# A new written order for the head of a retention-plus-gated-MLP kernel: blocks first, V products in four steps, splitting shared out over three engines

## The chip, the core and the metric

The kernel runs on one core of a Trainium2 chip. The metric is device time in microseconds of one execution. The kernel before has a median of 406.89 us over three runs (404.96 to 407.62). The profiled execution was a run of 406.76 us, whose span from the first to the last instruction is 404.8 us; the 1.96 us between them lie around the span.

## The reference

A linear attention with decay (retention) feeds a gated MLP that also mixes along the sequence:

```python
for t in range(S):          # q, k, v: 4 batches, 8 heads, 768 steps, 64 wide
    state = gamma * state + k[t] (x) v[t]
    y[t]  = scale * (q[t] @ state)
x   = y, heads side by side                       # 4 x 768 x 512
h   = relu(x @ w_in);  u, v = halves of h         # 512 wide each
v_n = (v - mean) / sqrt(var + 1e-6)
v_s = w_spatial @ v_n + b_spatial                 # along the 768 steps
out = (u * v_s) @ w_out
```

The weights `w_in` and `w_out` come as float64. On the chip each is split into a high and a low part, and every product of that stage is three matmuls (high by high, high by low, low by high).

## The kernel before, in words

Each batch has six **groups** of 128 steps. A group `g` is loaded by `load_group` (word `G`, two DMAs of 512 KB into a `qv` tile, three buffers). Its scores are `s` (`q`, 32 small matmuls in the trace), masked on VectorE into `ws` (`j`); its values are scaled by the decay (`p`, GpSimd); in the first batch a running sum of k by v is kept in the PSUM tile `total` (`t`) and copied out by ScalarE (`k`); `y` makes the output products `x`; `E` brings them out of PSUM on VectorE into `xf`; `h` makes the high half `xh` (ScalarE) and `l` the low half `xl` (GpSimd).

The **weights** come in twelve blocks of 128 x 512: four of the V half of `w_in` (`winv_w`), four of its U half (`winu_w`), four of `w_out` (`wout_w`). `L` loads one (512 KB), `a` takes the absolute value on ScalarE, `c0`, `c1` and `c2` are five VectorE instructions (lines 180 to 200: two, two and one) that build the float32 parts, `H` writes the high part (ScalarE), and `R` the low part (`split_residue`). For blocks 0 and 1 `R` is three matmuls with an identity matrix into a PSUM tile `rud`, which ScalarE copies out (`A`); for the other blocks it is two GpSimd instructions (lines 132 and 217). A block lives in one of four `room` tiles while it is split.

For each of six row chunks there is a **V product** `V`: twelve matmuls in a row over the four blocks of `winv_w`. Then `r` (relu, ScalarE), `s` (statistics, VectorE), `w` (power -0.5, GpSimd), `n` (bias, VectorE) and `N` (normalised into `vnh`, ScalarE). All six `N` must be there before the first **spatial product** `sp` (lines 507 to 513). The MLP then goes through eight **units** (four column blocks by two halves): a U product `u` of twelve matmuls, `sp`, the gate (`t` on VectorE twice, `gh` on ScalarE, `gl` on GpSimd, lines 535 to 538), and the output product `o` of nine matmuls.

The **order** of the first batch's head is written by hand: `START` is a string of such words, emitted in that order, and with `fixed` set every instruction keeps its place on its engine. `START` of the kernel before ends with the two U products `u1` and `u0` and the last normalisation. Then comes `FIRST`, which holds the splitting of blocks 6 to 11 (`C6` to `C11`, six steps in one word) between the units (`I0` to `I7`) and the groups of the next batch (`S`, `X`, `G`). In `FIRST` the matmuls and the loads keep the written order and the scheduler places the rest. All loads are on SyncE's one queue, in the written order.

Of the kernel before, what the change touches and what calls it, by code (L numbers as in the profile page):

```python
# [9 lines left out]
F32 = mybir.dt.float32  # L10
# [13 lines left out]
START = (  # L24
    "v m L0 e G0 L1 L2 G1 L3 G2 L4 a0 c00 c01 q0 p0 c02 H0 j0 R0 a1 c10 t00 a2 y00 k00 c11 A0 t01 "
    "c20 y01 G3 L5 H1 k01 E0 q1 p1 j1 h0 a3 l0 t10 k10 c30 y10 t11 c21 y11 G4 K0 k11 p2 q2 E1 H2 a4 "
    "j2 h1 t20 l1 k20 c31 t21 y20 k21 p3 q3 c12 H3 y21 G5 K1 K2 L6 L7 B j3 R1 E2 t30 A1 c32 y30 h2 "
    "p4 k30 q4 c22 a5 t31 j4 y31 G6 k31 R2 t40 E3 k40 t41 c40 h3 R3 y40 k41 c50 q5 y41 j5 p5 V0 c41 "
    "c51 l2 H4 V1 r0 l3 c42 H5 E4 R4 t50 r1 c52 y50 k50 s1 V2 h4 R5 L8 L9 L10 L11 K3 K4 K5 s0 y51 "
    "r2 l4 V3 E5 w0 s2 h5 w1 l5 n0 n1 V4 N0 w2 r3 N1 n2 s3 N2 V5 w3 r4 n3 s4 N3 w4 u1 r5 n4 N4 s5 "  # L30
    "w5 u0 n5 N5"
)
FIRST = (
    "C6 C7 I0 C8 C9 I1 G7 Z5 C10 I2 S6 C11 G8 I3 X6 S7 G9 I4 X7 S8 W0 G10 I5 X8 S9 W1 G11 I6 X9 "
    "S10 W2 G12 V0 V1 I7 X10 S11 G13 N0 V2 N1 V3 N2 X11 G14 V4 N3 V5 N4 O7 N5"
)
# [10 lines left out]

BLOCKS = [0, 1, 2, 3, 4, 5, 6, 8, 7, 9, 10, 11]
STAGED = {i: (("vnh", "vnl")[i // 3], i % 3) for i in range(6)}
STAGED |= {i: ("vnl", i - 8) for i in range(8, 11)}  # L50
UNIT_BLOCKS = 2
WARM_UP = 10
# [3 lines left out]
def tile_retention_gmlp(  # L56
# [8 lines left out]
    mask: bass.AP,  # L65
    eye: bass.AP,
    vdecay: bass.AP,
# [4 lines left out]
    nc = tc.nc  # L72
# [23 lines left out]
    mask_t = wpool.tile([P, C], F32, name="mask_t")  # L96
    eye_t = wpool.tile([P, P], F32, name="eye_t")
    minus_t = wpool.tile([P, P], F32R, name="minus_t")
    vd_t = wpool.tile([P, NC, 2, NP], F32, name="vd_t")
# [28 lines left out]
    def load(dst, src):  # L128
        tc.keep_in_program_order(nc.sync.dma_start(dst, src))  # L129
# [3 lines left out]

    def pick(on_vector):
        return nc.vector if on_vector else nc.gpsimd

# [4 lines left out]
    ]  # L141
    doubles = [doubles[i] for i in BLOCKS]
    raws = {}

    def load_eye():
        load(eye_t, eye)
        keep(nc.scalar.mul(minus_t, eye_t, -1.0))

# [22 lines left out]
    def split_top(i):  # L171
        parts = raws.pop(i).bitcast(I32).rearrange("p (n w) -> p n w", w=2)
        a = rooms[i % 4] if fixed else rpool.tile([P, DM], F32, tag="xf", name=f"da{i}")[:, :]
        tc.keep_in_program_order(nc.scalar.activation(a, parts[:, :, 1].bitcast(F32), AF.Abs))
        halves[i] = [a, None, parts]
# [28 lines left out]

    def split_residue(i):
        hi, lo, _ = doubles[i]
        a, f, _ = halves.pop(i)
        if i < UNIT_BLOCKS:

            ps = ps_m.tile([P, DM], F32, tag="m", name=f"rud{i}")  # L210
            mm(ps, eye_t, f, start=True, stop=False)
            mm(ps, eye_t, a, start=False, stop=False)
            mm(ps, minus_t, hi, start=False, stop=True)
            halves[i] = ps
        else:
            keep(residue(nc.gpsimd, f, f, hi))
            keep(nc.gpsimd.tensor_tensor(lo, f, a, ALU.add))  # L217

    def split_copy(i):
        keep(nc.scalar.copy(doubles[i][1], halves.pop(i)))  # L220

    def split_double(i):
        for step in (split_top, split_exponent, split_sign, split_low, split_high, split_residue):
            step(i)

# [38 lines left out]

    def scale_values(g):
        vd = vd_t[:, g % NC].unsqueeze(3).broadcast_to([P, 2, NP, D])
        tc.keep_in_program_order(nc.gpsimd.tensor_tensor(values[g], values[g], vd, ALU.mult))  # L267

# [81 lines left out]
    def out_products(g, i):  # L350
        c = g % NC
        if i == 0:
            pool, tag = (ps_o, "o") if fixed else (ps_m, "m")
            outs[g] = [
                pool.tile([P, NP // 2, 2, C], F32, tag=tag, name=f"x{g}_{n}") for n in range(2)
            ]
        ts = outs[g]
        both = c > 0 or i > 0

        def part(hp, kept):  # L360
            w, m = (states, queries) if kept else (values, scores)
            for r in range(2):
                rows = place(hp, r)
                mm(
                    ts[hp % 2][ROWS[r], hp // 2, i],
                    w[g][rows, i, hp],
                    m[g][rows, i, hp],
                    start=not kept,
                    stop=bool(kept or not both),
                )  # L370

        for hp in range(0, NP, 2):
            for kept in range(1 + both):
                for n in range(2):
                    part(hp + n, kept)
        if i == 1:
            for kind in (queries, keys, values, naturals, scores):
                del kind[g]

# [20 lines left out]

    def out_half(g, low):
        b, c = divmod(g, NC)
        xh, xl = xhalf[b, c // TT]
        cols = slice((c % TT) * P, (c % TT) * P + P)
        if low:
            keep(residue(nc.gpsimd, xl[:, :, cols], outs.pop(g), xh[:, :, cols]))
        else:
            keep(nc.scalar.copy(xh[:, :, cols], outs[g]))  # L408
# [7 lines left out]

    def split3(pairs, ps):
        n = len(pairs)
        i = 0
        for (ah, al), (bh, bl) in pairs:  # L420
            for l, r in ((ah, bh), (ah, bl), (al, bh)):
                mm(ps, l, r, start=(i == 0), stop=(i == 3 * n - 1))
                i += 1
# [3 lines left out]

    def v_products(b, c):
        if b not in vn:
            vn[b] = [  # L430
                mpool.tile([P, NC, DM], F32R if b else F32, tag=tag, name=f"{tag}{b}", bufs=1)
                for tag in (("vnh", "vnl") if b else ("vnh",))
            ]
        xh, xl = xhalf[b, c // TT]
        cols = slice((c % TT) * P, (c % TT) * P + P)
        ps = ps_m.tile([P, DM], F32, tag="m", name=f"v{b}_{c}")
        split3(
            [
                ((xh[:, k, cols], xl[:, k, cols]), (winv_h[:, k], winv_l[:, k]))
                for k in range(KT)  # L440
            ],
            ps,
        )
        norm[b, c] = ps

# [60 lines left out]

    def mlp_spatial(b, j, half):
        dcol = slice(j * P, j * P + P)
        pp = ps_m.tile([P, DM], F32, tag="m", name=f"sp{b}_{j}_{half}")
        if b == 0:  # L510
            for s in range(NC):
                l, r = vn[b][0][:, s, dcol], whole_sp[half, s // 2][:, s % 2]
                mm(pp[:, :HALF], l, r, start=(s == 0), stop=(s == NC - 1))
        else:
            vh, vl = vn[b]
            split3(
                [
                    (
                        (vh[:, s, dcol], vl[:, s, dcol]),
                        (wsp_h[:, half, s], low_sp[half, s // 2][:, s % 2]),  # L520
                    )
                    for s in range(NC)
                ],
                pp[:, :HALF],
            )
        t = mpool.tile([P, HALF], F32, tag="t", name=f"t{b}_{j}_{half}")
        gh = mpool.tile([P, HALF], F32R, tag="gh", name=f"gh{b}_{j}_{half}")
# [39 lines left out]
    def item(b, i):  # L567
        if i == 0:
            mlp_u(b, *units[0])
        if i + 1 < NU:  # L570
            mlp_u(b, *units[i + 1])
        mlp_spatial(b, *units[i])
        if i > 0:
            mlp_out(b, *units[i - 1])
# [6 lines left out]
        "L": lambda b, g, n: load_double(n),  # L581
        "C": lambda b, g, n: split_double(n),
        "W": lambda b, g, n: split_spatial(n),
# [5 lines left out]
        "v": lambda b, g, n: [load(vd_t, vdecay), load(qg_t, qgroup), load(qd_t, qdecay)],  # L589
        "e": lambda b, g, n: load_eye(),  # L590
        "B": lambda b, g, n: load(bsp_t, b_sp),
        "q": lambda b, g, n: ret_scores(n),
        "p": lambda b, g, n: scale_values(n),
        "j": lambda b, g, n: ret_mask(n),
# [4 lines left out]
        "h": lambda b, g, n: out_half(n, False),  # L599
        "l": lambda b, g, n: out_half(n, True),  # L600
        "V": lambda b, g, n: v_products(0, n) if fixed else mlp_v(b + 1, n),
        "r": lambda b, g, n: v_relu(0, n),
# [6 lines left out]
        "H": lambda b, g, n: split_high(n),  # L609
        "R": lambda b, g, n: split_residue(n),  # L610
        "A": lambda b, g, n: split_copy(n),
    }

# [5 lines left out]
    nc.vector.memset(wz, 0.0)  # L619
    wps = ps_o.tile([P, DM], F32, tag="o", name="wps")  # L620
    for i in range(WARM_UP):
# [87 lines left out]
```

## Time and profile before

| what | value |
|---|---|
| median of three runs | 406.89 us (404.96 to 407.62) |
| the profiled execution | 406.76 us |
| its span | 404.8 us |
| instructions | 10218 |
| TensorE clock granted, mean | 0.977 |
| data moved | 41.55 MB |
| end of the third output product `o2` | 102.59 us |

The profile is one execution. A window row gives, for a stretch of the span, the busy microseconds of each engine, the granted TensorE clock and what the DMA engines did. A row of the chain of waits gives a start, a length and what the end of the program was waiting for then: a matmul row on TensorE followed by another means that TensorE ran on. A group row gives a line, an engine, an operation, the tiles, the count, busy microseconds and the mean of one in nanoseconds, and then the idle time just ahead of it.

### The profile page before, as it was taken

The numbers are of one execution on the slowest core, as the hardware profiler recorded it, in microseconds if no ns is written. First come the engines' busy times: TensorE is split into PE (matmuls) and PEld (weight loads), VectorE is DVE, ScalarE is ACT, GpSimd is POOL, SyncE is SP. The second block draws the span as 40 slices with busy tenths as digits, with TensorE's granted clock in tenths as the row PEclk, the third lists the DMA queues.
The fourth block names the chain that finished last, engine by engine and source line by source line (L and its number), as shares of the span: only waits on it lengthen the run. The fifth ranks groups of instructions, "written<-read, shape, count | busy, mean of one in ns | idle before, by whom it ended". The sixth has DMA issues, their size and how long they took to land.

```text
span 404.8 us, 10218 instructions
## 1 busy us (share of the span) xinstructions
PE 383.6 (95%) x4452; PEld 328.3 (81%) x4452; DVE 202.9 (50%) x433; ACT 127.6 (32%) x231; POOL 133.9 (33%) x128
## 2 busy tenths in 40 slices
PE   4976997799999998999999999999999999999996
PEld 2656785577777876899999988999999888999995
DVE  1799745997455665455543244454443246121122
ACT  2533355223132244622222144521132146311212
POOL 0359722667333333233333221243332222012010
PEclk8798999699999999999999999999999999999999
DMA  7989390000353314233335300233310000100202
GB/s 232 407 319 361 128 405 26 1 1 2 105 185 105 106 55 156 79 105 107 105 105 184 105 2 1 79 105 107 105 59 24 1 0 27 54 2 0 78 2 78
DMA packets 14012, 41.55 MB, mean 103 GB/s; under 512 B 1936, under 2 KB 2320, under 8 KB 13968
## 3 DMA queue, kind: packets, MB, share of 16 engines
q1 hardware_dynamic: 13968, 40.90, 28.5%
q8 instruction: 35, 0.57, 0.6%
q14 instruction: 9, 0.07, 0.1%
HBM read 34.61 MB, written 6.29 MB: 101 GB/s over the span
## 4 chain that ended last, share of the span: by engine, by line
PE 90%; ACT 2%; issue 2%; DVE 2%; POOL 1%; DMA 1%; SPq 1%; ACTq 0%; POOLq 0%
PE sp L124 26%; PE u L124 17%; PE o L124 16%; PE v L124 16%; PE x L124 6%; PE s L124 3%; PE d L124 3%; PE rud L124 1%; PE total L124 1%; DMA qv<-in_groups_dram 1%; DVE xf L391 1%; SPq L129 1%; ACT xh L408 0%; ACT vr L480 0%; POOL df L132 0%
## 5 line engine op out<-in xcount | busy, mean ns | idle before, releaser
L124 PE MATMUL u<-xh,winu_w 128*128 128x384 f32 x256 | 73.2, 349 | 4.9 <-POOL winu_w L217 3.9
L132 POOL TENSOR_TENSOR gl<-t,gh 128x384 fp32r<-128x384 f32 x31 | 32.3, 1042 | 132.8 <-ACT gh L537 124.6
L535 DVE TENSOR_TENSOR t<-sp,bsp_t 128x384 f32<-128x384 f32 (+1 forms) x34 | 18.0, 533 | 94.9 <-PE sp L124 94.9
L124 PE MATMUL o<-wout_w,gh 128*128 128x512 f32 x192 | 62.0, 404 | 0.0
L124 PE MATMUL v<-winv_w,xh 128*128 128x512 f32 x192 | 60.7, 397 | 0.6 <-ACT xh L408 0.6
L124 PEld LDWEIGHTS u<-xh,winu_w 128*128 128x128 f32 x256 | 47.5, 191 | 7.4 <-POOL winu_w L217 4.2
L124 PE MATMUL sp<-wsp_h,vnl 128*128 128x384 f32 x144 | 48.1, 334 | 0.0
L124 PE MATMUL sp<-wsp_h,vnh 128*128 128x384 f32 x144 | 48.1, 334 | 0.0
L124 PE MATMUL sp<-wsp_l,vnh 128*128 128x384 f32 x144 | 48.1, 334 | 0.0
L132 POOL TENSOR_TENSOR xl<-xf,xh 128x512 fp32r<-128x512 f32 x24 | 32.0, 1333 | 42.7 <-ACT xh L408 42.5
L537 ACT CAST gh<-t 128x384 fp32r<-128x384 f32 (+1 forms) x34 | 16.6, 493 | 92.6 <-DVE t L536 92.2
L124 PE MATMUL u<-xl,winu_w 128*128 128x384 f32 x128 | 43.5, 340 | 0.0
L124 PEld LDWEIGHTS v<-winv_w,xh 128*128 128x128 f32 x192 | 35.9, 190 | 8.7 <-ACT xh L408 1.0
L124 PEld LDWEIGHTS o<-wout_w,gh 128*128 128x128 f32 x192 | 35.8, 188 | 7.6
L391 DVE SCALAR_TENSOR_TENSOR xf<-x,qg_t,qd_t 128x128 f32<-128x128 f32 x96 | 27.0, 343 | 27.8 <-PE x L124 27.7
L124 PE MATMUL v<-winv_w,xl 128*128 128x512 f32 x96 | 37.7, 393 | 0.6 <-POOL xl L132 0.6
L124 PE MATMUL o<-wout_w,gl 128*128 128x512 f32 x96 | 37.7, 393 | 0.0
L124 PE MATMUL sp<-wst,vnh 128*128 128x384 f32 x96 | 33.6, 502 | 0.0
L267 POOL TENSOR_TENSOR qv<-qv,vd_t 128x512 f32<-128x512 f32 x24 | 28.4, 1182 | 15.7 <-DMA raw<-in_w_inv_dram 9.7
L124 PE MATMUL s<-qv 64*64 64x64 f32 x768 | 28.8, 226 | 4.0 <-DMA qv<-in_groups_dram 4.0
L124 PEld LDWEIGHTS s<-qv 64*64 64x64 f32 x768 | 26.2, 140 | 5.9 <-DMA qv<-in_groups_dram 4.4
L455 DVE BATCH_NORM_STATS2 bst<-vr 128x6 f32<-128x512 f32 x24 | 16.6, 693 | 28.6 <-ACT vr L448 28.6
(75 smaller groups left out, 623.6 us busy)
## 6 DMA issues: line engine op xcount, KB each, us to landing
qv<-in_groups_dram SPq DMA_DIRECT2D x48, 512.0 KB, 5.3
out_dram<-ot SPq DMA_DIRECT2D x23, 256.0 KB, 2.1
wst<-in_w_sp_dram SPq DMA_DIRECT2D x6, 384.0 KB, 7.4
raw<-in_w_inv_dram SPq DMA_DIRECT2D x4, 512.0 KB, 7.7
raw<-in_w_inu_dram SPq DMA_DIRECT2D x4, 512.0 KB, 7.6
raw<-in_w_out_dram SPq DMA_DIRECT2D x4, 512.0 KB, 7.7
bsp_t<-in_b_sp_dram SPq DMA_DIRECT2D x1, 384.0 KB, 8.8
qd_t<-in_qdecay_dram SPq DMA_DIRECT2D x1, 256.0 KB, 2.7
```

The source lines that it names most:

```text
L124: ins = nc.tensor.matmul(out, lhs, rhs, start=start, stop=stop, skip_group_check=shared)
L129: tc.keep_in_program_order(nc.sync.dma_start(dst, src))
L132: return eng.tensor_tensor(out, whole, high.bitcast(F32), ALU.subtract)
L267: tc.keep_in_program_order(nc.gpsimd.tensor_tensor(values[g], values[g], vd, ALU.mult))
L391: nc.vector.scalar_tensor_tensor(xf[:, hp], t[hp % 2][:, hp // 2].rearrange("p i c -> p (i c)"), qg_t[:, c, hp : hp + 1], qd_t[:, hp], ALU ...
L455: keep(nc.vector.bn_stats(st, norm[b, c][0]))
L535: nc.vector.tensor_tensor(t[:, c], pp[:, c], bsp_t[:, tc_], ALU.add)
L537: nc.scalar.copy(gh[:, c], t[:, c])
```

## The change

The strings `START` and `FIRST` are written anew. `START` now goes on until the third output product `o2` and the splitting of block 11, with the words `P` (a spatial product alone), `g` (the two VectorE steps of the gate), `f` (its high half, ScalarE), `d` (its low half, here always VectorE) and `o`. `FIRST` begins at the fifth unit. A word's first digit names the engine for `p`, `l`, `R` and `d`: 0 GpSimd, 1 VectorE, 2 ScalarE for `p` and `l`, and `R20` to `R31` are blocks 0 to 11 on VectorE.

- The identity, its negative, the two `rud` groups of matmuls and the copies `A` are gone. Blocks 0 and 6 to 11 get their residue on VectorE (two `TENSOR_TENSOR` each), blocks 1 to 5 on GpSimd.
- The decay scaling of group 0 is on VectorE, of group 1 on GpSimd, and of groups 2 to 6 on ScalarE as eight `ACTIVATE` of 128 x 64 each. The low halves of groups 1, 2 and 5 are on VectorE.
- The three gates inside the head have their low half on VectorE, and so has the fourth.
- `V` takes one block at a time: `V21` is chunk 2 with block 1, three matmuls. The steps of three chunks are placed between the score and output products of groups 2 to 5.
- The first load is block 0, then group 0, then the decay tables and the mask. The blocks are no longer permuted.
- The warm-up matmuls write to a tile of another PSUM pool.
- Of the next batch's groups, the score products of group 7 and the fifth U product come after `o2`; before, they came ahead of it.

```diff
-    "v m L0 e G0 L1 L2 G1 L3 G2 L4 a0 c00 c01 q0 p0 c02 H0 j0 R0 a1 c10 t00 a2 y00 k00 c11 A0 t01 "
...
+    "L0 G0 a0 c00 c01 H0 v c02 p10 m q0 L2 j0 t00 k00 y00 y01 t01 R20 G1 L1 p1 a2 G2 c20 E0 q1 h0 "
...
-    "C6 C7 I0 C8 C9 I1 G7 Z5 C10 I2 S6 C11 G8 I3 X6 S7 G9 I4 X7 S8 W0 G10 I5 X8 S9 W1 G11 I6 X9 "
...
+    "S6 I4 X6 S7 G9 W0 I5 X7 S8 G10 W1 I6 X8 S9 G11 W2 V0 V1 I7 X9 S10 G12 N0 V2 N1 V3 N2 X10 S11 "
...
-    def split_residue(i):
+    def split_residue(i, engine=None):
         hi, lo, _ = doubles[i]
         a, f, _ = halves.pop(i)
-        if i < UNIT_BLOCKS:
-
-            ps = ps_m.tile([P, DM], F32, tag="m", name=f"rud{i}")
-            mm(ps, eye_t, f, start=True, stop=False)
-            mm(ps, eye_t, a, start=False, stop=False)
-            mm(ps, minus_t, hi, start=False, stop=True)
-            halves[i] = ps
-        else:
-            keep(residue(nc.gpsimd, f, f, hi))
-            keep(nc.gpsimd.tensor_tensor(lo, f, a, ALU.add))
+        engine = engine or nc.gpsimd
+        keep(residue(engine, f, f, hi))
+        keep(engine.tensor_tensor(lo, f, a, ALU.add))
...
-    def scale_values(g):
+    def scale_values(g, engine=None):
+        engine = engine or nc.gpsimd
+        if engine is nc.scalar:
+            for i in range(2):
+                for hp in range(NP):
+                    v, f = values[g][:, i, hp], vd_t[:, g % NC, i, hp : hp + 1]
+                    keep(nc.scalar.mul(v, v, f))
+            return
...
-    def v_products(b, c):
+    def v_products(b, c, ks=range(KT)):
...
+        if not ks[0]:
+            norm[b, c] = ps_m.tile([P, DM], F32, tag="m", name=f"v{b}_{c}")
         split3(
-            [
-                ((xh[:, k, cols], xl[:, k, cols]), (winv_h[:, k], winv_l[:, k]))
-                for k in range(KT)
-            ],
-            ps,
+            [((xh[:, k, cols], xl[:, k, cols]), (winv_h[:, k], winv_l[:, k])) for k in ks],
+            norm[b, c],
+            start=not ks[0],
+            stop=ks[-1] == KT - 1,
         )
...
+        "R": lambda b, g, n: split_residue(n % 20, pick(n // 20)),
+        "P": lambda b, g, n: spatial_products(0, *units[n]),
+        "g": lambda b, g, n: gate_product(0, *units[n]),
+        "f": lambda b, g, n: gate_high(0, *units[n]),
+        "d": lambda b, g, n: gate_low(0, *units[n % 10], pick(n // 10)),
+        "o": lambda b, g, n: mlp_out(0, *units[n]),
```

How the order on the engines changes is shown at three places. The first is TensorE around the first V products (`v0_c` is chunk c, `x4_n` and `s5` are output and score products of groups 4 and 5, `rud` the identity products, `total` the running sum). The kernel before:

```order
L124 MATMUL rud1_429<-df1_185,eye_t_74 128x512
L124 MATMUL rud1_429<-room1_89,eye_t_74 128x512
L124 MATMUL rud1_429<-winv_w_82,minus_t_75 128x512
...
L124 MATMUL s5_570<-qv5_417 64x64 x16
L124 MATMUL x4_0_549<-ws4_308,qv4_307 64x64 x2
...
L124 MATMUL v0_0_606<-winv_w_82,xh0_222 128x512 x2
L124 MATMUL v0_0_606<-winv_w_82,xl0_223 128x512
```

The kernel after, from the scores of group 2 on:

```order
L122 MATMUL s2_298<-qv2_194 64x64 x16
L122 MATMUL s3_324<-qv3_267 64x64 x16
L122 MATMUL total_141<-qv2_194 64x64 x8
L122 MATMUL v0_0_362<-winv_w_80,xh0_200 128x512 x2
L122 MATMUL v0_0_362<-winv_w_80,xl0_201 128x512
...
L122 MATMUL s4_424<-qv4_355 64x64 x16
L122 MATMUL total_141<-qv3_267 64x64 x8
L122 MATMUL v0_1_459<-winv_w_80,xh0_200 128x512 x2
L122 MATMUL v0_1_459<-winv_w_80,xl0_201 128x512
...
L122 MATMUL s5_542<-qv5_522 64x64 x16
```

The identity products are gone, and a step of three V matmuls stands behind the scores of group 2, where the V products before began behind those of group 5.

The second place is the splitting of the later blocks. Before, GpSimd made their low parts between the gates:

```order
L132 TENSOR_TENSOR df7_886<-df7_886,wout_w_85 128x512
L217 TENSOR_TENSOR wout_w_85<-df7_886,da7_882 128x512
L132 TENSOR_TENSOR df8_911<-df8_911,winu_w_83 128x512
L217 TENSOR_TENSOR winu_w_83<-df8_911,da8_907 128x512
L132 TENSOR_TENSOR df9_922<-df9_922,wout_w_85 128x512
```

After, VectorE makes them in line with its other steps (`t` is a gate, `gl` its low half; lines 130 and 203 are the two residue steps):

```order
L193 SCALAR_TENSOR_TENSOR room0_86<-raw8_676,room0_86 128x512
L130 TENSOR_TENSOR df8_953<-df8_953,wout_w_83 128x512
L203 TENSOR_TENSOR wout_w_83<-df8_953,room0_86 128x512
L514 TENSOR_TENSOR t0_0_0_969<-sp0_0_0_946,bsp_t_77 128x384
L515 TENSOR_TENSOR t0_0_0_969<-t0_0_0_969,ur0_0_0_905 128x384
L184 SCALAR_TENSOR_TENSOR df10_976<-raw8_676,room2_88 128x512
L188 TENSOR_SCALAR room2_88<-df10_976 128x512
L130 TENSOR_TENSOR gl0_0_0_982<-t0_0_0_969,gh0_0_0_979 128x384
```

Two VectorE steps per block and one per gate are new there, and GpSimd has nothing between the last power of the normalisation and group 7.

The third place is SyncE's queue of loads behind group 6, after the change (`wst` is a piece of the spatial weights):

```order
L127 DMA qv6_666<-in_groups_dram 128x1024 x2
L127 DMA raw8_676<-in_w_out_dram 128x512
L127 DMA wst0_688<-in_w_sp_dram 128x768
...
L127 DMA raw7_85<-in_w_inu_dram 128x512
L127 DMA wst2_800<-in_w_sp_dram 128x768
L127 DMA bsp_t_77<-in_b_sp_dram 128x768
...
L127 DMA wst3_972<-in_w_sp_dram 128x768
```

`raw8` shares its buffer with blocks 3 to 5, so it waits for them to be split, and the first three pieces of the spatial weights, which stood ahead of such a wait before, now stand behind it.

## The prediction on record

> **What bounds the kernel now.** I read a table of windows first, cut where the work changes: the groups, the V products, the first unit, units two and three, the rest.
>
> ```profile
> core 0: us, PE busy (x) PEld busy (x) DVE busy (x) ACT busy (x) POOL busy (x), PEclk, DMA share, GB/s
> ...
> 8.87:40.09 31.22, 24.84 (x667) 19.66 (x667) 28.32 (x47) 12.02 (x25) 17.68 (x14) 0.88 0.96 363
> 40.09:59.51 19.42, 19.42 (x154) 15.68 (x154) 12.60 (x34) 8.55 (x14) 11.12 (x12) 0.96 0.69 261
> 59.51:76.62 17.11, 12.24 (x50) 9.98 (x49) 11.43 (x18) 6.44 (x11) 6.59 (x6) 0.87 0.11 45
> 76.62:102.59 25.97, 25.97 (x188) 18.36 (x189) 21.46 (x30) 7.80 (x15) 17.11 (x13) 0.95 0.00 1
> 102.59:404.80 302.21, 297.38 (x3393) 263.42 (x3393) 128.43 (x306) 90.64 (x164) 81.07 (x80) 1.00 0.22 75
> ```
>
> TensorE is the bound: 302.21 us after the third output product run almost without a hole, and the change leaves that work as it is. What can move is the head, up to 102.59. In the first row VectorE is busy 28.3 of 31.2 us and the DMA engines 0.96, while TensorE has holes; in the third TensorE stands still for 4.9 us. The view of TensorE's waits names the holes:
>
> ```profile
> PE s L124 <- DMA qv<-in_groups_dram: 4.0, 1, 4.0
> PE u L124 <- POOL winu_w L217: 3.9, 1, 3.9
> PE x L124 <- issue: 2.5, 1, 2.5
> ...
> PE total L124 <- issue: 1.6, 1, 1.6
> ```
>
> The first group's load, and a weight block that was split too late; "issue" is TensorE waiting for nothing that the profile shows.
>
> The chain of waits gives the price of each piece where it runs undisturbed, and of three that do not (the first `s`, the first `rud`, the `u` at 73.05):
>
> ```profile
> 3.53 5.29 DMA qv<-in_groups_dram
> ...
> 8.87 1.97 PE s L124 x32
> 10.84 3.88 PE rud L124 x5
> ...
> 24.86 0.62 PE total L124 x14
> ...
> 27.59 2.15 PE rud L124 x5
> ...
> 30.82 0.93 PE s L124 x32
> ...
> 32.22 0.47 PE x L124 x30
> ...
> 51.12 8.39 PE v L124 x36
> ...
> 73.05 3.57 PE u L124 x10
> ...
> 84.97 2.30 PE u L124 x12
> 87.28 3.87 PE sp L124 x12
> 91.14 2.09 PE o L124 x9
> ```
>
> Up to `o2` the kernel before has 8 `s` at 0.93 (7.4), 11 `total` at 0.62 (6.8), 12 half groups of `x` at 0.5 (6.0), 6 V chunks at 8.39/3 = 2.8 (16.8), 5 `u` at 2.30 (11.5), 4 `sp` at 3.87 (15.5), 3 `o` at 2.09 (6.3), and `rud` 3.88 + 2.15 (6.0): 76.3 us. From 8.87 to 102.59 are 93.7 us, so **17.4 us are lost**. By window: 8.4 among the groups, 1.0 in the V products, 6.3 from 59.51 to 76.62 (17.1, where two `u`, one `sp` and a third `u` make 10.8), 1.6 after.
>
> **The change part by part.** *Start.* Block 0 and group 0 are now the first three loads of a queue that issues one in some 0.45 us:
>
> ```profile
> 0.74 0.38 SPq L129 DMA_DIRECT2D vd_t<-in_vdecay_dram  x1
> 1.17 0.42 SPq L129 DMA_DIRECT2D qg_t<-in_qgroup_dram  x1
> ```
>
> The first half of group 0 takes the second place, at 1.2 us. With the 5.29 us to landing above, scores start at 6.5 instead of 8.87: 2.4 us.
>
> *TensorE work.* Up to `o2` it now has 7 `s`, 4 `u` and no `rud`: 6.5 + 6.8 + 6.0 + 16.8 + 9.2 + 15.5 + 6.3 = 67.1 us. The scores of group 7 (with the state product between them, 1.1) and the fifth `u` (2.3) are left for later; that is postponed and gains nothing. So with L for the time lost after the start, `o2` ends at 6.5 + 67.1 + L, and the span is 73.6 + L + 3.4 + 302.2 = 379.2 + L.
>
> *What L becomes.* Among the groups V steps fill holes, but the chain scores, mask, `x`, eviction is as long as it was and VectorE has more to do, so I keep the 8.4 us. The late block goes: blocks 4 and 5 are split ahead of the `u`, 6 and 7 well ahead of theirs; of 6.3 I keep 1.0, for the normalisation of the last chunk. Of the 1.6 after, 0.5 stays. In the V products 1.0 stays. ScalarE now scales groups 2 to 6 ahead of `total`. No row has a 128 x 64 `ACTIVATE`; the nearest are these:
>
> ```profile
> L289 ACT COPY ws<-total 128x256 f32<-128x256 f32 x11 | 4.1, 371 | 6.6 <-PE total L124 6.5
> L147 ACT ACTIVATE minus_t<-eye_t 128x128 fp32r<-128x128 f32 x1 | 0.3, 309 | 5.6 <-DMA eye_t<-in_eye_dram 5.6
> ```
>
> At most 8 x 0.309 = 2.5 us a group; with the slope between the rows (0.062 for 128 columns) 8 x 0.278 = 2.2. I take 2.3, against 1.13 on GpSimd. ScalarE has 12.0 busy of 31.2 us there, and `s` and V steps stand ahead of most of the sums: 1.0 us in all, between 0 (hidden) and 5 x 1.2 = 6. That makes L = 8.4 + 1.0 + 1.0 + 0.5 + 1.0 = **12**, and `o2` at 85.6. (The Trainium skill, "ScalarE: Activation LUTs", section "What ACT_TABLE_LOAD costs", gives 186 ns + 0.833 ns per column, 93 more for a pointer operand and 93 overlapped back to back: an estimate of 2.0 us a group, which would change the sum by nothing above 0.3 us a group.)
>
> *VectorE*, the second view of the same end. It takes residues of seven blocks and must keep up. Its prices, up to `o2`, and over the run for line 132:
>
> ```profile
> L200 DVE SCALAR_TENSOR_TENSOR room<-raw,room 128x512 f32<-128x512 uint32 x6 | 7.5, 1256 | 0.0
> L391 DVE SCALAR_TENSOR_TENSOR xf<-x,qg_t,qd_t 128x128 f32<-128x128 f32 x24 | 6.7, 341 | 3.6 <-PE x L124 3.5
> L309 DVE TENSOR_TENSOR ws<-s,mask_t 128x512 f32<-128x512 f32 x8 | 5.5, 682 | 1.1 <-PE d L124 1.0
> L182 DVE TENSOR_SCALAR room<-room 128x512 int32<-128x512 int32 x6 | 5.2, 862 | 0.2
> L180 DVE TENSOR_SCALAR room<-room 128x512 f32<-128x512 f32 x6 | 4.8, 806 | 8.0 <-ACT room L174 8.0
> L195 DVE TENSOR_SCALAR room<-df 128x512 int32<-128x512 int32 x6 | 4.5, 748 | 0.2
> L191 DVE SCALAR_TENSOR_TENSOR df<-raw,room 128x512 int32<-128x512 int32 x6 | 4.4, 727 | 0.1
> ...
> L455 DVE BATCH_NORM_STATS2 bst<-vr 128x6 f32<-128x512 f32 x6 | 4.1, 691 | 4.7 <-ACT vr L448 4.7
> ```
> ```profile
> L132 DVE TENSOR_TENSOR vnl<-vr,vnh 128x512 fp32r<-128x512 f32 x18 | 12.8, 725 | 9.2 <-ACT vnh L481 9.2
> ```
> ```profile
> 78.79 0.43 DVE L195 TENSOR_SCALAR da<-df 128x512 int32<-128x512 int32 x1
> 79.25 0.69 DVE L200 SCALAR_TENSOR_TENSOR da<-raw,da 128x512 f32<-128x512 uint32 x1
> 80.04 1.31 DVE L180 TENSOR_SCALAR da<-da 128x512 f32<-128x512 f32 x1
> ```
> ```profile
> 79.48 1.59 POOL L132 TENSOR_TENSOR df<-df,winu_w 128x512 f32<-128x512 f32 x1 [1.74 <-ACT winu_w L203]
> ```
>
> Undisturbed, a block's five steps cost 0.43 + 0.43 + 0.69 + 0.43 + 0.69 = 2.67 us; the means of blocks 0 to 5 add up to 4.40. The step at 80.04 shows why: it ends 0.28 us after GpSimd's instruction, three times its own length. Blocks 0 to 5 lost 10.4 us to some 28 us of GpSimd work. Until the third gate's low half VectorE now has the blocks but for the end of the last (30.2), 12 residue steps at 0.725 (8.7), 7 masks (4.8), six evictions (6.7), three low halves and one scaling (2.9), statistics and biases (some 7.3, 4.1 of it the row above), gates (3 x 3 x 0.55 = 5.0): 65.6 us. GpSimd has 18 us left beside it (14 steps near 1.3), at the same share 6.7 more. From about 6 us, with 4 us of waits, that ends at 82.3, and `o2` 2.4 later at 84.7. The two views agree within 1 us: both engines are nearly full, and VectorE has no slack left to give. (The Trainium skill, "SBUF — State Buffer", section "SBUF: two separate sides", calls the port pair of the two engines an exclusive lock, held for a whole instruction; the two rows agree.)
>
> *Queues.* `raw8` waits until VectorE ends block 5, at about 44 (from 6: six blocks 16.0, a residue, masks, evictions and the rest 13, the GpSimd share 6, waits 3). Behind it on SyncE stand the spatial weights, which land some 7 us after their issue:
>
> ```profile
> wst<-in_w_sp_dram SPq DMA_DIRECT2D x6, 384.0 KB, 7.4
> ```
>
> With six transfers in a row I allow 10 us, so 54, and the first `sp` comes near 58 (6.5, then 36.1 of groups and V products, 10.4 lost, two `u` 4.6). `wst3` to `wst5` wait for rooms that blocks 8 to 10 free near 76 and land by 84; the fifth `sp` comes past 90. I cost both at nothing; without that cover each is worth up to one landing, 7.4 us.
>
> **Sum.** 379.2 + 12 = 391.2 us of span, and 406.76 - 404.8 = 1.96 around it: **393.2 us**, against 406.76 of the profiled execution and a median of 406.89.
>
> **Rivals.**
> - *The lost time only moves.* L stays 17.4, because VectorE is late everywhere instead of one block once: 398.6. For it: 28.3 of 31.2 us busy already. Against: the 3.9 us wait is of one place that is gone.
> - *The holes are really filled.* The group stage loses only the two "issue" gaps (4.1) and L is 5: 386.2. For it: eight V steps stand there now. Against: TensorE waits in order, so a step helps only where its own inputs are earlier than the next score.
> - *VectorE stays in GpSimd's way.* If all twelve blocks cost 4.40, VectorE has 20.8 less 6.7 us more than I gave it, `o2` ends at 98.8 and the time is 406.4: no change. Against: beside blocks 6 to 11 GpSimd now has almost nothing.
> - *The clock falls (the slower side).* After the 3.9 us wait the `u` at 73.05 took 3.57 us for 10 of its 12 (4.3 against 2.30, 1.86 times), and the first `s` 1.97 against 0.93. If chopped V steps and short waits keep TensorE at that pace through groups and V products, V costs 14.4 and scores 7.2 us more: 414.8. It decides from about 14 us, where the gain is eaten. Against: the clock in the second window is 0.88 with holes of up to 2.5 us. (The Trainium skill, "TensorE: Matmul & The Clock Gate", section "What's actually happening", drops the clock after an idle window of about 3.4 us; by that the 3.9 us wait cost its slow stretch, which the trace shows, and the holes left would not.)
>
> **How the numbers follow.** Forecast 0.52; the lost time moves 0.22; holes filled 0.12; VectorE in the way 0.09; clock 0.05. Faster by over 1% (below 402.8, about what a measurement here can tell) are the first three: 0.86; within 1% the fourth, 0.09; slower 0.05. The range reaches to the filled holes below, and above past the moved loss toward the fourth: 386 to 402.
>
> **What would show it.** Right: scores start near 6.5; no `rud`; VectorE over 85% busy from 10 to 80; blocks 6 to 11 at 2.7 us each with GpSimd quiet; no wait on `winu_w` over 1 us; `o2` at 83 to 88; the stretch behind it as long as before. Wrong: `sp` waiting for `wst`, a granted clock under 0.9 from 40 on, VectorE's waits for TensorE growing, or over 2 us lost in the next batch, whose groups now run one place later.

## The result

The changed kernel takes 386.77 us (median of 4 runs, 386.46 to 387.37) against 405.92 of the kernel before on the same chip (4 runs, 404.57 to 407.62): a ratio of 0.9528, with a 95% interval of 0.9484 to 0.9572. Forecast were 393.2, in a range of 386 to 402. The profiled execution took 386.46 us, its span is 384.7, so 20.1 us less than before.

**The profile after.** The table of windows, cut where the work changes: the start, the groups (now with the V products of chunks 0 to 2 in them), the V products of chunks 3 to 5, the first four units up to `o2`, the rest.

```profile
core 0: us, PE busy (x) PEld busy (x) DVE busy (x) ACT busy (x) POOL busy (x), PEclk, DMA share, GB/s
...
5.50:41.30 35.80, 30.07 (x806) 25.57 (x805) 33.69 (x65) 22.19 (x64) 14.35 (x11) 1.00 0.77 291
41.30:49.69 8.39, 8.39 (x38) 6.96 (x38) 7.44 (x21) 6.42 (x16) 7.16 (x8) 1.00 0.83 272
49.69:79.77 30.08, 30.08 (x127) 22.27 (x129) 27.80 (x56) 12.29 (x22) 2.86 (x4) 1.00 0.49 171
79.77:384.70 304.93, 300.73 (x3469) 266.35 (x3469) 131.96 (x314) 92.50 (x167) 81.15 (x79) 1.00 0.21 74
```

TensorE is busy in every instant from 41.30 to 79.77, and its granted clock is 1.00 in every row, where before it was 0.88, 0.96, 0.87 and 0.95 in the four windows of the head. (Three of the four executions have a mean clock of 1.000; the fourth, 387.37 us, has 0.985.) VectorE is now the other full engine: 33.69 of 35.80 us, then 27.80 of 30.08.

The view of TensorE's waits, which showed 4.0 for the first group, 3.9 for `winu_w` and two "issue" gaps:

```profile
PE s L122 <- DMA qv<-in_groups_dram: 1.9, 3, 0.8
PE total L122 <- POOL qv L253: 1.7, 1, 1.7
PE total L122 <- DVE qv L253: 1.5, 1, 1.5
...
```

The wait on a weight block is gone. What is left in the head lies almost all ahead of 20 us: from there to the end of the groups TensorE is idle for 0.44 us.

```profile
5.50:20.00 14.50, 9.22 (x309) 8.27 (x310) 13.97 (x29) 6.51 (x18) 2.87 (x2) 1.00 1.03 396
20.00:41.30 21.30, 20.86 (x501) 17.30 (x499) 19.72 (x38) 15.68 (x47) 11.48 (x9) 1.00 0.59 221
```

The chain of waits from the last group on, with the third output product ending at 77.69 + 2.08 = 79.77 (102.59 before):

```profile
41.30 8.38 PE v L122 x36
49.69 4.18 PE u L122 x24
53.87 15.48 PE sp L122 x48
69.35 2.08 PE o L122 x9
71.43 2.09 PE u L122 x12
73.52 2.08 PE o L122 x9
75.60 2.09 PE u L122 x12
77.69 2.08 PE o L122 x9
```

Each row begins where the one ahead of it ends. The units' stage is pure matmul time.

**Where the 20.1 us came from**, by the boundaries of both profiles: the first scores start at 6.10 instead of 8.87 (2.8); from there to the first `u` it is 43.6 instead of 50.6 us (7.0; the `rud` work stood there for 6.0 before, but what its removal is worth is a question for the experiments); from the first `u` to the end of `o2` 30.1 instead of 43.1 us (13.0); behind that 304.9 instead of 302.2 (2.7 given back: the postponed `u`, scores and state product are 3.4, and 0.7 was gained at places that I did not trace).

### The profile page after: what moved, and what is told of

It is laid out like the page before. It is cut to its first block, busy times and chain, and to the rows that moved or that the text cites. A ratio compares the mean times of both kernels' runs of the same rounds, so it can differ in the third digit from the quotient of the medians.

```text
span 384.7 us, 10219 instructions
## 1 busy us (share of the span) xinstructions
PE 373.6 (97%) x4442; PEld 322.5 (84%) x4442; DVE 201.2 (52%) x455; ACT 135.3 (35%) x268; POOL 105.8 (28%) x105
## 4 chain that ended last, share of the span: by engine, by line
PE 88%; DVE 6%; DMA 3%; issue 1%; ACT 1%; POOL 1%; DVEq 0%; POOLq 0%; ACTq 0%
PE sp L122 28%; PE u L122 18%; PE o L122 17%; PE v L122 15%; PE x L122 5%; PE d L122 3%; PE s L122 2%; DMA qv<-in_groups_dram 2%; DVE xf L374 1%; DMA raw<-in_w_inv_dram 1%; DVE room L173 1%; DVE room L188 1%; DVE df L184 1%; PE total L122 1%; DVE room L175 1%
## 5 line engine op out<-in xcount | busy, mean ns | idle before, releaser
L122 PE MATMUL u<-xh,winu_w 128*128 128x384 f32 x256 | 71.4, 342 | 0.0
L130 POOL TENSOR_TENSOR gl<-t,gh 128x384 fp32r<-128x384 f32 x27 | 28.1, 1039 | 157.4 <-ACT gh L544 149.0
L542 DVE TENSOR_TENSOR t<-sp,bsp_t 128x384 f32<-128x384 f32 (+1 forms) x30 | 15.8, 531 | 94.2 <-PE sp L122 94.2
L122 PEld LDWEIGHTS u<-xh,winu_w 128*128 128x128 f32 x256 | 46.7, 188 | 1.5
L544 ACT CAST gh<-t 128x384 fp32r<-128x384 f32 (+1 forms) x30 | 14.5, 491 | 84.8 <-DVE t L543 84.5
L130 POOL TENSOR_TENSOR xl<-xf,xh 128x512 fp32r<-128x512 f32 x21 | 28.0, 1335 | 39.9 <-ACT xh L391 39.8
L122 PE MATMUL sp<-wst,vnh 128*128 128x384 f32 x96 | 31.8, 486 | 0.0
L122 PE MATMUL s<-qv 64*64 64x64 f32 x768 | 27.5, 221 | 1.9 <-DMA qv<-in_groups_dram 1.9
L122 PEld LDWEIGHTS s<-qv 64*64 64x64 f32 x768 | 25.2, 136 | 4.2 <-DMA qv<-in_groups_dram 2.1
L391 ACT CAST xh<-xf 128x512 fp32r<-128x512 f32 x24 | 14.9, 620 | 37.5 <-DVE xf L374 37.3
```

The source lines that it names most:

```text
L122: ins = nc.tensor.matmul(out, lhs, rhs, start=start, stop=stop, skip_group_check=shared)
L130: return eng.tensor_tensor(out, whole, high.bitcast(F32), ALU.subtract)
L542: nc.vector.tensor_tensor(t[:, c], pp[:, c], bsp_t[:, tc_], ALU.add)
L544: nc.scalar.copy(gh[:, c], t[:, c])
```

## The experiments

Each run is compared with the kernel before by its ratio, and with the changed kernel's 386.77 by its median. The changed kernel's own executions span 0.9 us, and the medians of the kernel before in the other comparisons lie within 0.4 us of the 405.92 above, so a difference of less than about 1 us says nothing. Where stages are compared, it is profile against profile, one execution each.

### The unit stage: the late block, and the clock behind it

**Block 6 early, in the kernel before.** One move in the old order (and block 6 keeps the buffer that it had):

```
START: ... V4 N0 [+ a6 c60 c61] w2 r3 N1 n2 [+ c62 H6] s3 N2 V5 ... N3 w4 [+ R6] u1 r5 ...
FIRST: [- C6] C7 I0 C8 C9 I1 ...
```

> The kernel before with one edit: the seventh block (the one whose lateness held up the third u for 3.9 us) is split some 10 us earlier, inside the head, on the same engines; all the rest of the old order stays. Theory (the unit stage lost its time to that one late block and to the slow clock behind it): 3.9 + 3 = 6 to 7 us faster than before, 398 to 400, so nearly half of the whole gain of the change. Rival (the next blocks are as late, the wait moves to blocks 7 and 8, since VectorE and GpSimd split them in each other's way): 1 to 3 us faster, 402 to 405, with a new wait of TensorE on a weight block.

Measured: 399.29 us, ratio 0.9824 (0.9783 to 0.9864): 7.0 us less than the 406.24 of before beside it. The units' window (five `u` here, as before) and what is left of waits on weight blocks in it:

```profile
57.45:94.35 36.90, 35.58 (x235) 26.03 (x237) 30.21 (x46) 13.45 (x25) 23.39 (x19) 1.00 0.13 53
```
```profile
PE o L124 <- POOL wout_w L217: 0.8, 2, 0.5
...
PE u L124 <- POOL winu_w L217: 0.5, 1, 0.5
```

Before, the same stretch took 43.08 us; it lost 6.2, as the theory had it. (This span is 8.4 shorter; the other 2 us lie ahead of the units, 1.4 of them ahead of the move: in this execution the groups ended at 38.73 instead of 40.09, with a hole of 1.71 us where it was 2.55, and the clock did not fall behind it.) The next blocks are late too, but by 1.3 us in all. So one late block, moved alone, is worth about a third of the whole gain: 6.2 of 19.1 us.

**The same wait filled with work, in the kernel before.**

```
         pu = ps_m.tile(...)
+        if b == 0 and half == 0 and j == 2:
+            for _ in range(24):
+                mm(pu[:, :HALF], winu_h[:, 0, :P], xh[:, 0], start=True, stop=True)
```

> The kernel before with 24 extra products of unit 0's weights into the third u's tile ahead of its own, some 4 us of TensorE work in the place of the 3.9 us wait; they are overwritten, so the result is the same. Theory (the wait itself and the slow stretch behind it are two losses: the u at 73.05 and the sp at 76.6 took some 3 us more than the same work elsewhere): with no standstill the slow stretch goes, 2 to 3 us faster than before, 402.5 to 404, and the granted clock stays at 1 there. Rival (the slow stretch has another cause, or the wait alone is the loss): 405 to 407, no change.

Measured: 404.14 us (10 runs), ratio 0.995 (0.9924 to 0.9977), so 2.1 us less although TensorE was given some 3 us more to do. The same two windows, the wait and what follows it, first of the kernel before, then of this one; the column behind the engines is the granted clock:

```profile
69.14:73.05 3.91, 0.00 (x0) 0.00 (x0) 3.88 (x3) 0.48 (x1) 3.86 (x3) 0.91 0.00 0
73.05:79.00 5.95, 5.95 (x15) 4.74 (x16) 5.66 (x8) 1.41 (x3) 2.93 (x2) 0.50 0.00 1
```
```profile
69.14:73.05 3.91, 2.87 (x18) 2.55 (x16) 3.88 (x3) 0.38 (x1) 3.81 (x3) 1.00 0.00 0
73.05:79.00 5.95, 5.95 (x24) 4.32 (x25) 5.66 (x8) 1.47 (x3) 2.91 (x2) 1.00 0.00 1
```

After the standstill the clock is at half for 6 us, in which 15 products get done; without it 24 do. (Of the wait 1.0 us stays empty.) From the block's arrival to the end of `o2` it is 27.0 us here (73.01 to 100.03) and 29.5 in the kernel before. The late block cost its wait and, behind it, some 2.5 us by the slow clock.

**The residues of blocks 6 to 11 and the gates' low halves on GpSimd again.** `R26 R28 R29 R30 R27 R31` become `R6 R8 R9 R10 R7 R11`, and `d10` to `d13` become `d0` to `d3`.

> The changed kernel with the residues of blocks 6 to 11 and the low halves of gates 0 to 3 on GpSimd again. Theory (VectorE has slack in the unit stage, since TensorE runs there without a hole; the steps taken from VectorE, 12 x 0.69 + 4 x 0.55 = 10.5 us, pay for the 6 us that GpSimd's work beside it costs): within 1% of the changed kernel, 386 to 389. Rival (GpSimd's place beside the blocks is what made them late before: their five steps go from 2.67 back to 4.40 us, six times 1.7 = 10.4, of which VectorE gets the 10.5 of residues back, but each residue takes 2.7 instead of 1.4 us, and a u or an output product waits for it): 391 to 396, with a wait on a weight block over 1 us.

Measured: 390.37 us, ratio 0.9594 (0.9569 to 0.9620), 3.6 slower than the changed kernel: too slow for the theory, just under the rival's range, and not by its wait either. No weight block is late; a gate's low half is, which stands behind the residues on GpSimd. TensorE's longest wait, and the windows around it:

```profile
PE o L122 <- POOL gl L130: 2.3, 1, 2.3
```
```profile
74.07:76.38 2.31, 0.00 (x2) 0.00 (x1) 2.21 (x3) 0.12 (x1) 2.31 (x3) 0.97 0.33 69
76.38:79.40 3.02, 3.02 (x7) 2.44 (x8) 0.36 (x1) 0.13 (x1) 2.78 (x2) 0.50 0.95 362
```

2.3 us of wait and 3 us at half clock, worth 1.5: that is 3.8 of the 4.0 us by which this span is longer. The move of residues and low halves to VectorE is worth this much, through the place in a queue and not through the blocks' own price. The two were moved together: what either is worth alone is not shown.

### The groups: who sets their length

**The V products whole again.** The twelve steps `V00` to `V23` stand together ahead of `a6`; all else as changed.

> The changed kernel with the V products of chunks 0 to 2 in one piece again: their twelve steps stand together where the last of chunk 0 stood, all else as changed. In the changed kernel eight of them run between 20 and 33 us, 0.68 us each. Theory (the steps fill holes of TensorE that VectorE's chain leaves, so out of their places they come on top): up to 8 x 0.68 = 5.4 us slower than the changed kernel's 386.8, so 389 to 392, and TensorE idle among the groups by as much more. Rival (the group stage is as long as VectorE's work, wherever TensorE's steps stand, and the twelve steps still fit ahead of its end): within 1 us, 386 to 388.

Measured: 391.68 us, ratio 0.9621 (0.9583 to 0.9659), 4.9 slower. From the chain, the twelve steps and the three chunks behind them (41.30 in the changed kernel):

```profile
35.66 8.43 PE v L122 x36
...
46.56 8.39 PE v L122 x36
```

The last three chunks start 5.3 us later, about the length of eight steps. In their place TensorE has a new hole,

```profile
PE x L122 <- issue: 2.0, 1, 2.0
```

and behind it the granted clock stands at 0.50 from 29 to 35.5 us. How the 5.3 divides between the steps and the clock is not told apart in this execution. The other three have a mean clock of 0.995 or 0.996; as an estimate, that leaves room for some 4 us at half clock, so for a loss of 2 us. They took 390.35 to 392.68 us, 3.6 to 5.9 more than the changed kernel, so at least 1.6 us are the place of the steps.

**The clamps of blocks 2 to 5 three times.**

```
-        tc.keep_in_program_order(nc.vector.tensor_scalar(a, a, TOP_MAX, TOP_MIN, ALU.min, ALU.max))
+        for _ in range(3 if 2 <= i < 6 else 1):
+            tc.keep_in_program_order(
+                nc.vector.tensor_scalar(a, a, TOP_MAX, TOP_MIN, ALU.min, ALU.max)
+            )
```

> The changed kernel with the clamp of blocks 2 to 5 run three times instead of once on VectorE (it changes nothing the second time): 8 more steps of 0.43 us, 3.4 us of VectorE work among the groups and nothing else. Theory (VectorE's chain sets the length of the group stage): 3 to 5 us slower, 390 to 392. Rival (TensorE's own order and the loads set it, VectorE has slack): within 1 us, 386 to 388.

Measured: 390.66 us, ratio 0.9622 (0.9591 to 0.9653), 3.9 slower; in the profile the groups end at 46.31 instead of 41.30:

```profile
5.50:46.31 40.81, 33.28 (x806) 28.99 (x805) 36.62 (x73) 22.27 (x64) 13.75 (x11) 0.87 0.69 254
```

3.4 us more on VectorE alone make the stage 5.0 us longer in this execution, the slowest of the four, with a clock of 0.87 in the window. Another of the four had a mean clock of 1.000 and took 389.46 us, 2.8 more than the changed kernel's executions at 1.000 (386.71, their median). So at full clock most of the 3.4 us arrives, and VectorE has next to no slack here. What is above that in the 5.0 may be the clock; it was not told apart.

**Later scores.** The words `v` and `m` (the decay tables and the mask) stand between `L0` and `G0`.

> The changed kernel with the decay tables and the mask loaded ahead of the first group, as before; block 0 stays first. The first scores come four issues later, some 1.9 us. Theory (the group stage is as long as VectorE's work, which starts with block 0, untouched): the groups end at most 0.5 us later, 386 to 388. Rival (the prediction's start term: scores that start later end later by as much): 1.9 us, 388 to 389.5, the groups' end near 43.2 instead of 41.3.

Measured: 387.59 us, ratio 0.9548 (0.9522 to 0.9574), whose interval holds the changed kernel's ratio: the 0.8 us between the medians are not clear of noise. In the profiles, first the changed kernel's and then this one, the scores start at 8.06 instead of 6.10, and the groups end 1.0 later, at 42.29:

```profile
6.10 1.35 PE L122 MATMUL s<-qv 64*64 64x64 f32 x32 [0.47 <-DMA qv<-in_groups_dram]
8.06 1.15 PE L122 MATMUL s<-qv 64*64 64x64 f32 x32 [2.42 <-DMA qv<-in_groups_dram]
```

In this pair half of the 2.0 us arrives: between the two expectations.

**The first group ahead of block 0.** `L0 G0` becomes `G0 L0`, and `p1` becomes `p11`.

> The changed kernel with the first group loaded ahead of block 0 and group 1 scaled on VectorE instead of GpSimd, an attempt to take away the first two waits (1.5 and 1.7 us of TensorE for scaled values). If these waits set the end: 1 to 2 us faster, 385 to 386. If VectorE does: it starts two issues (0.9 us) later and has 0.69 us more, less 0.4 from GpSimd: 1.2 us slower, 387.5 to 388.5.

Measured: 389.11 us (6 runs), ratio 0.9577 (0.9541 to 0.9614), 2.3 slower, and more than either expectation. VectorE's first step waits for block 0 until 8.04, where it was 5.46 in the changed kernel, which is the first row:

```profile
5.46 0.43 DVE L173 TENSOR_SCALAR room<-room 128x512 f32<-128x512 f32 x1 [4.32 <-ACT room L167]
8.04 0.43 DVE L173 TENSOR_SCALAR room<-room 128x512 f32<-128x512 f32 x1 [6.91 <-ACT room L167]
```

VectorE starts 2.6 us later and the last three V chunks 2.2 later (at 43.45). The expectation had 0.9 for the two issues; the block, issued at 1.65 instead of 0.74, also took 5.7 us to land instead of 4.0. Here the load that VectorE needs first is the one to issue first; the second edit, the scaling, was not run alone.

**The `rud` work put back.** The identity products for blocks 0 and 1 in the place of `R20` and `R1`, with a load `e` behind the third block's:

```
+        if i < 2:
...
+            mm(ps, eye_t, f, start=True, stop=False)
+            mm(ps, eye_t, a, start=False, stop=False)
+            mm(ps, minus_t, hi, start=False, stop=True)
...
+            keep(nc.scalar.copy(lo, ps))
+            return
```

> The changed kernel with the residues of blocks 0 and 1 made by identity products on TensorE again (with the load of the identity, its negative and the copy out on ScalarE). Before, these two took TensorE 6.0 us in all, 4.3 undisturbed. Theory (TensorE's holes among the groups are set by VectorE, so such work disappears in them, and VectorE is relieved of 1.4 us): within 1 us of the changed kernel's 386.8, 386 to 388. Rival (the prediction's sum: what TensorE is given is added to the end): 4.3 to 6 us slower, 391 to 393.

Measured: 393.15 us, ratio 0.9678 (0.9645 to 0.9711), 6.4 slower, but by neither reason: ScalarE stood behind its copy of the first `rud`, and VectorE behind ScalarE:

```profile
17.22 0.43 DVE L180 TENSOR_SCALAR room<-room 128x512 f32<-128x512 f32 x1 [7.78 <-ACT room L174]
```

So the run says only what a queue costs. A second run has the load behind the third group's, and `M`, `R20`, `A0` and `A1` (negative, products, copies) just ahead of the first V steps that need them.

> The residues of blocks 0 and 1 by identity products once more, now placed so that no queue stands behind them: the identity is loaded after the third group, its negative made and the products and copies put just ahead of the first V step that needs them (in the run before, VectorE stood still for 7.8 us behind ScalarE's copy of the first). Theory (TensorE's holes among the groups take such work): within 1.5 us of the changed kernel's 386.8, 386 to 388.5. Rival (what TensorE is given is added to the end): 4.3 to 6 us slower, 391 to 393.

Measured: 388.96 us, ratio 0.9571 (0.9534 to 0.9609), 2.2 slower. The two `rud`, the first V steps behind them (20.53 in the changed kernel) and the last three chunks:

```profile
20.39 2.15 PE rud L125 x5
...
23.15 2.15 PE rud L125 x5
...
25.30 0.70 PE v L125 x3
...
44.07 8.39 PE v L125 x36
```

The V steps are 4.8 us late at 25.30, the chunks 2.8 late at 44.07: the holes that follow take back 2.0. Well placed, putting the work back costs 2.2 us, not 6.0 and not nothing. That is net: the residue steps of block 0 leave VectorE and those of block 1 GpSimd.

### Who scales, who subtracts

**Groups 2 to 6 scaled on GpSimd.** `p22` to `p26` become `p2` to `p6`.

> The changed kernel with the values of groups 2 to 6 scaled on GpSimd (one instruction of 1.13 us) instead of ScalarE (eight of 0.34, some 2.0 us a group). The prediction priced ScalarE's longer scaling at 1.0 us on the path; by that it would be 1 us faster, 385 to 386.3. Rival (ScalarE has room, and GpSimd's work lengthens VectorE's by 0.37 us for each of its own): 5 x 1.13 x 0.37 = 2.1 us slower, 388 to 390.

Measured: 389.94 us, ratio 0.9608 (0.9579 to 0.9637), 3.2 slower: the rival's sign, within its range, and more than the 2.1 us of its sum. VectorE's steps do get longer: up to the third gate's low half its `df`, second `room` and `xl` groups (lines 184, 193 and 130, 26 steps in both kernels) take 20.4 us by their rows instead of 17.7.

**Three small pieces back on GpSimd.** `R20`, `l11`, `l12` become `R0`, `l1`, `l2`.

> The changed kernel with three pieces of the group stage back on GpSimd: the residue of block 0 and the low halves of groups 1 and 2. VectorE loses 4 steps of 0.69 = 2.8 us of its own; GpSimd gets 4 of 1.3 = 5.2 us. Theory (VectorE sets the group stage, and each us of GpSimd costs it 0.37): 2.8 - 1.9 = 0.9 us faster, 385.5 to 386.5. Rival (the chain through these pieces matters more than VectorE's load: a low half takes 1.3 instead of 0.7 us and V waits for it, and GpSimd's scaling of group 1 comes later): 1 to 3 us slower, 388 to 390.

Measured: 387.82 us (6 runs), ratio 0.9544 (0.9510 to 0.9577), whose interval holds the changed kernel's ratio: no difference that can be told. The profile shows one thing that neither theory named. VectorE's scaling of the first group, 0.69 us in the changed kernel, meets the residue on GpSimd, and the first sums come 1.1 us later for it (10.01 instead of 8.91). The changed kernel's step, then the two of this run:

```profile
8.18 0.69 DVE L253 TENSOR_TENSOR qv<-qv,vd_t 128x512 f32<-128x512 f32 x1
```
```profile
7.83 1.58 POOL L130 TENSOR_TENSOR df<-df,winv_w 128x512 f32<-128x512 f32 x1 [7.00 <-ACT winv_w L196]
```
```profile
8.35 1.61 DVE L253 TENSOR_TENSOR qv<-qv,vd_t 128x512 f32<-128x512 f32 x1
```

None of the edits to the changed kernel beats it.

## Why the prediction was right in sign and too high in time

The span was forecast as 379.2 + L with L = 12; it is 379.2 + 5.5. Most of the mechanisms stand; L was over-sized in nearly every term. The time came out at the rival "the holes are really filled" (386.2), but not by that rival's account, which left 4.1 us in two "issue" gaps: those gaps are gone, and 7.5 us are lost among the groups. Of the signs that the forecast named, `o2` at 83 to 88 failed (79.77); VectorE's share from 10 to 80 (64.8 of 70 us), the weight blocks in time and the clock of 1.00 from 40 on came as it said.

**Start.** 6.5 forecast, 6.10 measured. But the sum passed every us of it on to the end, and the profile of the run with later scores passes on only half: 1.0 of 2.0. What starts the stage as much is VectorE's first step, which the sum did not mention for itself.

**The groups** (8.4 kept, plus 1.0 for ScalarE's scaling, 9.4): measured are 35.2 us from the first score, of which 27.7 is work by the same prices, so 7.5 lost. Of these TensorE is idle for 5.3, nearly all of it ahead of the first V step at 20.53; in the other 2.2 it is busy for longer than the prices say. "Among the groups V steps fill holes, but the chain is as long as it was" was half right: eight steps do stand in holes (the run with whole V products costs 4.9, part of it by the clock), and behind 20 us no hole worth naming is left. VectorE keeps the rest: it is busy for 13.97 of the 14.50 us up to there, and the run with the clamps shows that it has no slack. The `rud` work that went was counted at 6.0 us; put back with care it cost 2.2. So the worth of TensorE's removed work was taken too large and the holes that would be left too, and the two errors partly cancel, which is luck. The scaling was taken at 2.3 us a group; the group of its instructions shows 10.1 / 5 = 2.0:

```profile
L250 ACT ACTIVATE qv<-qv,vd_t 128x64 f32<-128x64 f32 x40 | 10.1, 339 | 1.8 <-DMA qv<-in_groups_dram 1.8
```

That is what the estimate from the Trainium skill ("ScalarE: Activation LUTs", section "What ACT_TABLE_LOAD costs") gave. A loss of 1.0 us for it cannot be seen: giving the work to GpSimd costs 3.2 us.

**V products, the last chunk's normalisation, the rest** (1.0 + 1.0 + 0.5): nothing was lost, 8.39 us for three chunks and no idle instant before 79.77. The units' stage is even 0.9 us under its own price of 31.0, because four `u` were priced at 2.30 each, from rows that follow the 64-row products of the scores; behind 128-row products they take 2.09, as the rows of `u` above show. Together that is 1.0 + 1.5 + 0.9 = 3.4 us of the 6.5, the groups 1.9, the start 0.4 and the stretch behind `o2` 0.7 (304.93 against 305.6).

**The 6.3 us of the late block.** Right, and the largest single piece that an experiment shows: 6.2 us in the units' stage of the run that moves that block alone, 7.0 between the medians.

**VectorE's view.** It forecast the third gate's low half at 82.3; it ends at 77.17 + 0.55 = 77.7. VectorE begins at 5.46 and up to there is busy this long:

```profile
5.46:77.75 72.29, 66.56 (x956) 53.43 (x956) 67.10 (x138) 39.81 (x98) 24.37 (x21) 1.00 0.68 246
```

67.1 us, where 65.6 + 6.7 = 72.3 were forecast. The prices were right in sum: by groups of instructions, the same stretch adds up to 72.5. (One price by luck: 18 us of GpSimd work beside VectorE were to cost 0.37 us each, 6.7 in all. There are 24.4 us of it, and the blocks' 35 one-input steps take 6.8 us more than 0.43 each, so 0.28 per us.) The step that failed is the adding. Independent instructions overlap, as four neighbours of the timeline show:

```profile
56.25 0.42 DVE L173 TENSOR_SCALAR room<-room 128x512 f32<-128x512 f32 x1
56.71 0.43 DVE L175 TENSOR_SCALAR room<-room 128x512 int32<-128x512 int32 x1
57.05 0.42 DVE L173 TENSOR_SCALAR room<-room 128x512 f32<-128x512 f32 x1
57.51 1.15 DVE L175 TENSOR_SCALAR room<-room 128x512 int32<-128x512 int32 x1
```
```profile
57.05 1.31 POOL L253 TENSOR_TENSOR qv<-qv,vd_t 128x512 f32<-128x512 f32 x1 [3.69 <-DMA qv<-in_groups_dram]
```

The second needs the first's result and begins 0.46 after it; the third is of another block and begins 0.34 after the second, ahead of its end. Interleaved as they are now, VectorE's steps cost up to 0.1 us less than their rows. The fourth is the price of GpSimd beside it: 1.15 instead of 0.43, until 0.30 us after the end of GpSimd's step. It is the only such step from 49.69 to 79.77, where GpSimd has 2.86 us of work; that bears out "blocks 6 to 11 at 2.7 us with GpSimd quiet", but for one step of block 6 (1.41 us at 46.96) that ran beside a residue of block 5.

**Queues** were rightly costed at nothing: no TensorE wait names `wst`, and the fifth `sp` (85.24) finds its weights.

**The rivals.** That the lost time only moves, and that VectorE stays in GpSimd's way, did not happen. "The clock falls" did not happen in the profiled execution, but the reason that I gave against it does not hold. I leaned on the trace's 0.88 with holes of 2.5 us, and on the Trainium skill's page "TensorE: Matmul & The Clock Gate", section "What's actually happening", which lets the clock fall after an idle window of some 3.4 us. I took from it that shorter holes would not count. But the 0.88 had the counter-example in it: behind the 2.55 us hole in the groups of the kernel before, the clock is 0.54.

```profile
34.99:37.54 2.55, 0.00 (x1) 0.00 (x0) 2.52 (x3) 0.13 (x1) 2.55 (x3) 1.00 0.97 340
37.93:41.30 3.37, 3.37 (x66) 3.06 (x62) 3.20 (x5) 0.43 (x1) 2.36 (x2) 0.54 0.93 375
```

In the run with GpSimd's residues a wait of 2.31 us gave 3 us at a clock of 0.50 (the row above). In the run with the clamps, behind first waits of 0.47 and 1.62 us, 9.5 to 12.5 stands at half clock, where the changed kernel, with 0.47 and 1.46, has 1.00. Up to there the two kernels run the same steps: the first added clamp is at 11.19. And the run with GpSimd's residues, also the same up to there, has 1.00 with 1.01 and 1.58. A row of the timeline and the window behind it, first of the run with the clamps, then of the changed kernel, then of the run with GpSimd's residues:

```profile
8.87 0.88 PE L122 MATMUL total<-qv 64*64 64x64 f32 x16 [1.62 <-DVE qv L256]
```
```profile
9.50:12.50 3.00, 3.00 (x80) 2.86 (x78) 2.44 (x5) 1.04 (x2) 0.00 (x0) 0.50 1.02 416
```
```profile
8.91 0.68 PE L122 MATMUL total<-qv 64*64 64x64 f32 x16 [1.46 <-DVE qv L253]
```
```profile
9.50:12.50 3.00, 2.36 (x94) 2.11 (x92) 2.76 (x8) 1.07 (x2) 0.00 (x0) 1.00 1.02 416
```
```profile
8.90 0.68 PE L122 MATMUL total<-qv 64*64 64x64 f32 x16 [1.58 <-DVE qv L253]
```
```profile
9.50:12.50 3.00, 2.27 (x90) 2.02 (x88) 2.49 (x6) 1.04 (x2) 0.00 (x0) 1.00 1.02 418
```

The measurement decides: holes of 1.6 to 2.55 us can halve the clock here. But the length of the hole does not settle it. The run with whole V products, with 0.82 and 1.57, stood at half clock from 8.5 to 11.5. One and the same kernel shows both: the four executions with the clamps have mean clocks from 0.982 to 1.000, the changed kernel's from 0.985 to 1.000. What decides it, these runs leave open. Up to 20 us the half clock cost next to nothing in the two pairs that show it, since TensorE waits there anyway (in the run with the placed `rud` it had the same slow stretch, and the `x` behind it began at 15.52 against 15.42; in the run with GpSimd's residues it was slow from 14.7 to 18.3, and the last V chunks began within 0.1 us of the changed kernel's); behind a hole in the units' stage it cost 1.5 to 2.5 us.

## What to carry to other kernels

Look first for the one late operand ahead of a dense stretch: its price is the wait and a slow stretch behind it, and moving that one piece gave 6 to 7 of 19 us. Cutting long TensorE work into steps placed into the holes of another engine's chain was worth some 5 us, but only while that other engine got no more to do: 3.4 us added to VectorE came back as 3.9 in the median. When an engine is nearly full, price it by its busy time over a stretch and not by the sum of its instructions' rows (67.1 against 72.5 us here), and ask of a step that is moved whose queue it will stand in, more than how long it takes.

## What the hardware showed that I had not expected

A hole of 2.3 us, or two of 0.5 and 1.6, can halve TensorE's clock for 3 us or more, in one execution and not in another. VectorE's instructions without a dependence overlap by some 0.1 us. A GpSimd step of 1.58 us stretched a two-input VectorE step from 0.69 to 1.61 us, as it stretches the one-input ones.
